# Pooled attention and a d_ff block on one core: the first two batches transposed on TensorE, first loads in another order, the first output phase in four banks

## The chip, the cores and the metric

The kernel runs on one NeuronCore of a Trainium2 chip. The metric is the device time of one execution in microseconds, the median of three runs. Before the change it is 352.62 us (352.56 to 353.64).

The engines are TensorE (PE: matmuls; its weight loads are shown as PEld), VectorE (DVE), ScalarE (ACT), GpSimd (POOL) and SyncE (SP). Each works through its own instructions in program order. Here SP only issues DMAs, and POOL issues some of them beside its arithmetic.

## The reference

Eight batches, eight heads, 576 tokens, head dimension 64; d_model 512 and d_ff 2048. Inputs and output are float32.

```python
k_p = k.reshape(B, H, 72, 8, D).mean(axis=3)      # pooled by 8 along the tokens
v_p = v.reshape(B, H, 72, 8, D).mean(axis=3)
scores = q @ k_p.T / sqrt(D)                      # 576 x 72 per batch and head
attn = softmax(scores)
x = (attn @ v_p), as 4608 x 512 (token, head*64+d)
h = x @ w_in                                      # 4608 x 2048
out = (h - tanh(h)) @ w_out                       # 4608 x 512
```

## The kernel before, in words

**Attention of one batch.** `load_kv` and `load_q` bring float32 rows into SBUF. `pool_kv` adds the eight token rows of a pool in three halvings; k's last step writes `kd`, a bf16 tile that holds every pooled row twice side by side, and v's last step multiplies with a block mask into `VB`. `q_prep` casts q to bf16 (L102 the 512 main tokens, L105 the last 64) and turns it with five DMA transposes (L109) into `qT`, where the head dimension lies on the partitions. `k_transpose` turns `kd` by matmuls with an identity operand into PSUM and copies it into `KB` (L167), a block layout with heads of even index on partitions 0 to 63 (copied by DVE) and of odd index on 64 to 127 (copied by ACT). `scores` multiplies `KB` with `qT` in two halves of 288 tokens and takes the exponential on ACT (L191). `av` multiplies a block of 128 tokens of it with `VB` (L208), whose last column per head gives the denominator; DVE takes its reciprocal (L217) and scales (L218) into `x_sb`; a DMA transpose (L226) writes that into `xT`, the input of the second part, with d_model on the partitions.

**The d_ff part** goes over nine groups of 512 tokens. Phase one, `mlp_h`, has sixteen steps, one per 128 columns of d_ff: four matmuls with 512 columns into an `hT_ps` bank (L256), tanh on ACT (L264), and the subtraction on DVE into a bf16 tile `gT` (L266). Phase two, `mlp_o`, has four blocks of 128 tokens (`tb`), each with four quarters (`qd`) of four matmuls (L276) that add into one `o_ps` bank; at the end of a block ACT copies it out (L285), and SP stores it. A batch has 576 tokens, a group 512, so group g needs the tokens of batches up to g alone.

**Order.** The schedule is manual: every engine runs its instructions in the order in which the program lists them. Ahead of the groups stand the loads of batch 0 on SP, identity, mask and memsets, `pool_kv(0)` with k on DVE and v on POOL, the cast loads of both weight matrices from POOL's queue (four pieces of `w1`, L322, then four of `w2`, L326), `q_prep(0)`, the loads of batch 1 on SP, and scores and `av` of batch 0. Inside group g the attention of batch g+1 is spread: its pooling on POOL at step 1, `q_prep` and the loads of batch g+2 at step 3, `k_transpose` at step 13, the five `scores` in the first five quarters of phase two, and the five `av` behind quarters 6, 7, 9, 10 and 12. SP's queue therefore holds, in order: loads of batch 0, q transposes of batch 0, loads of batch 1, x transposes of batch 0, and so on.

**PSUM** has eight banks: three for `hT_ps`, two for `o_ps`, and three (`ps_a`) that k transposes, scores and `av` share.

Of the kernel before, what the change touches and what calls it, by code (L numbers as in the profile page):

```python
# [33 lines left out]
def kernel(  # L34
# [64 lines left out]
    def q_prep(b):  # L99
        t = q_raws.pop(b)  # L100
        q_bf = work.tile([128, R + 1, H, D], BF16, name="q_bf", tag="q_bf")
        nc.vector.tensor_copy(  # L102
            out=q_bf[:, 0:R, :, :].rearrange("p j h d -> p h j d"), in_=t[:, :, 0:R, :]
        )
        nc.vector.tensor_copy(out=q_bf[:QT, R, :, :], in_=t[:QT, :, R, :])  # L105
# [9 lines left out]
    def pool_kv(b, ke, ve):  # L115
        kr = k_raw[b % 2].rearrange("p t (j d) -> p t j d", d=D)
        vr = v_raw[b % 2].rearrange("p t (j d) -> p t j d", d=D)
        kd = work.tile([128, NT, 2, D], BF16, name="kd", tag="kd")
        for eng, r in ((ke, kr), (ve, vr)):
            eng.tensor_tensor(  # L120
                out=r[:, :, 0:4, :], in0=r[:, :, 0:4, :], in1=r[:, :, 4:8, :], op=ALU.add
            )
            eng.tensor_tensor(  # L123
                out=r[:, :, 0:2, :], in0=r[:, :, 0:2, :], in1=r[:, :, 2:4, :], op=ALU.add
            )
            if r is kr:
                eng.tensor_tensor(  # L127
                    out=kd[:, :, :, :],
                    in0=r[:, :, 0:1, :].to_broadcast([128, NT, 2, D]),
                    in1=r[:, :, 1:2, :].to_broadcast([128, NT, 2, D]),  # L130
                    op=ALU.add,
                )
            else:
                eng.tensor_tensor(
                    out=r[:, :, 0, :], in0=r[:, :, 0, :], in1=r[:, :, 1, :], op=ALU.add
                )
                eng.tensor_tensor(  # L137
                    out=VB[b % 2][:, :, :, 0:D],
                    in0=r[:, :, 0:1, :].to_broadcast([128, NT, 3, D]),
                    in1=mask[:, :, :, :].to_broadcast([128, NT, 3, D]),  # L140
                    op=ALU.mult,
                )
        kdups[b] = kd

    def k_transpose(b):
        kd = kdups.pop(b)
        kb = KB[b % 2]
        for half in range(2):
            ps = ps_a.tile([128, 4, G], FP32, name="kT_ps", tag="ps_a")
            flat = ps.rearrange("p h g -> p (h g)")  # L150
            c = half * 4 * G
            while c < (half + 1) * 4 * G:
                t = c // 128
                n = min((t + 1) * 128, (half + 1) * 4 * G) - c
                nc.tensor.matmul(  # L155
                    flat[:, c - half * 4 * G : c - half * 4 * G + n],
                    lhsT=kd[:, t, :, :].rearrange("p a d -> p (a d)"),
                    rhs=ident[:, c - t * 128 : c - t * 128 + n],
                    start=True,
                    stop=True,  # L160
                )
                c += n
            for par, eng in ((0, nc.vector.tensor_copy), (1, nc.scalar.copy)):
                for i in range(2):
                    hp = half * 2 + i
                    hh = 2 * hp + par
                    eng(  # L167
                        out=kb[par * D : (par + 1) * D, hp, hh * G : (hh + 1) * G],
                        in_=ps[par * D : (par + 1) * D, 2 * i + par, :],
                    )  # L170
# [4 lines left out]
    def scores(b, t):  # L175
# [24 lines left out]
    def av(b, blk):  # L200
# [3 lines left out]
        x_sb = work.tile([128, 2, 4, D], BF16, name="x_sb", tag="x_sb", bufs=3)  # L204
        for half in range(2):
            ps = ps_a.tile([128, 4, D1], FP32, name="x_ps", tag="ps_a")
# [9 lines left out]
            rden = work.tile([128, 4, 1], FP32, name="rden", tag="rden", bufs=3)  # L216
# [71 lines left out]


    load_kv(0)  # L290
    load_q(0)
    make_identity(nc, ident)
    nc.gpsimd.memset(mask[:, :, :, :], 1.0)
# [7 lines left out]
        pattern=[[2 * G - 2 * G - 16 + 0, NT], [-G, 3]],  # L301
# [7 lines left out]
        base=G - 1 - G,  # L309
# [3 lines left out]
    for i in range(2):  # L313
        nc.vector.memset(k_raw[i][64:128, 4, :], 0.0)
        nc.vector.memset(v_raw[i][64:128, 4, :], 0.0)
        nc.vector.memset(KB[i][:, :, :], 0.0)
        nc.gpsimd.tensor_scalar_mul(VB[i][:, :, :, D:D1], mask[:, :, :, :], float(POOL))


    pool_kv(0, nc.vector, nc.gpsimd)  # L320
    for c in range(4):
        nc.gpsimd.dma_start(  # L322
            out=w1b[:, :, c * 512 : (c + 1) * 512], in_=w1_src[:, :, c * 512 : (c + 1) * 512]
        )
# [4 lines left out]
    q_prep(0)  # L329
    load_kv(1)  # L330
    load_q(1)
    k_transpose(0)
    for t in range(NT):
        scores(0, t)
    for blk in range(5):
        av(0, blk)


    for g in range(NG):
        nb = g + 1 if g + 1 < B else None  # L340
        gts = []
        for i in range(NHID):
            mlp_h(g, i, gts)
            if nb is not None:
                if i == 1:
                    pool_kv(nb, nc.gpsimd, nc.gpsimd)
                if i == 3:
                    q_prep(nb)
                    if nb + 1 < B:
                        load_kv(nb + 1)  # L350
                        load_q(nb + 1)
                if i == 13:
                    k_transpose(nb)
        for tb in range(4):
            for qd in range(4):
                mlp_o(g, tb, qd * 4, qd * 4 + 4, gts)
                u = tb * 4 + qd
                if nb is not None:
                    if u < NT:
                        scores(nb, u)  # L360
                    if u in (6, 7, 9, 10, 12):
                        av(nb, (6, 7, 9, 10, 12).index(u))
# [30 lines left out]
```

## Time and profile before

| | |
|---|---|
| median of 3 runs | 352.62 us (352.56 to 353.64) |
| the profiled execution's own time | 351.93 us |
| its span, first to last instruction | 350.2 us |
| PE busy | 287.7 us, 82% of the span |
| DVE, ACT, POOL busy | 166.7, 139.9, 106.9 us |
| first `hT` matmul of group 0 | 58.98 us |
| first `hT` matmul of group 1 | 94.44 us |
| mean granted TensorE clock | 0.961 |
| loads of one batch, page's issue part | k, v, q: 1152 KB each |
| weights | 4 pieces of 512 KB each in bf16 (twice that read as float32) |
| moved by DMA | 51.68 MB, of it 36.70 read from HBM |

All rows come from one profiled execution; times in them are microseconds from the start of the span. An arrow in a row's last part names what ended the idle time in front of that instruction. A matmul's end is modelled, so a busy PE is not PE at its peak; the distance between starts is the safer figure. The chain of waits is followed back from the last instruction: at each step to what released it.

### The profile page before, as it was taken

To read this page: it belongs to the slowest core of one execution; us is meant where nothing else is said; L and a number is where in the kernel's file an instruction comes from. 1 tells how busy PE (TensorE), PEld (TensorE's weight loads), DVE (VectorE), ACT (ScalarE), POOL (GpSimd) and SP (SyncE) were. 2 spreads that over 40 slices of the span, in tenths; PEclk is the share of its full clock that TensorE was granted. 3 is DMA by queue.
4 is the path that set the end of the run, shared out by engine and by line. 5 is a ranking of instruction groups with operands and counts; after the bars stand their busy time and mean duration, and the time that the engine had idled before them with its cause. 6 is when DMAs were issued, how large, how long until landed. Compare 5 with 4: busy or idle time off the path is not lost.

```text
span 350.2 us, 4472 instructions
## 1 busy us (share of the span) xinstructions
PE 287.7 (82%) x1538; PEld 143.3 (41%) x1568; DVE 166.7 (48%) x361; ACT 139.9 (40%) x293; POOL 106.9 (31%) x72
## 2 busy tenths in 40 slices
PE   0007002899989998999999899989998999999994
PEld 0004001345535543554455345535544554444442
DVE  6603002672485448355725772485458265703800
ACT  0023000464266246615551664266246615514611
POOL 2790940006800940193049007700940000000000
PEclk9999655899999999999999999999999999999999
DMA  6689995069827953892497469627952032012023
GB/s 240 179 139 282 265 219 98 16 121 329 171 73 212 286 119 69 259 254 83 104 321 169 95 176 311 146 48 232 281 104 67 22 89 79 2 60 61 2 51 69
DMA packets 71446, 51.68 MB, mean 148 GB/s; under 512 B 45312, under 2 KB 57600, under 8 KB 71424
## 3 DMA queue, kind: packets, MB, share of 16 engines
q1 hardware_dynamic: 67200, 47.20, 50.2%
q0 software_dynamic: 4224, 4.19, 7.4%
q8 instruction: 12, 0.20, 0.2%
q14 instruction: 10, 0.08, 0.1%
HBM read 36.70 MB, written 9.44 MB: 132 GB/s over the span
## 4 chain that ended last, share of the span: by engine, by line
PE 75%; DMA 9%; SPq 7%; DVE 5%; issue 2%; ACT 1%; ACTq 0%; DVEq 0%
PE o_ps L276 35%; PE hT_ps L256 31%; DMA xT<-x_sb 6%; PE s_ps L184 4%; PE x_ps L208 4%; SPq L91 3%; DMA q_raw<-in_q_dram 3%; DVE q_bf L102 3%; SPq L109 2%; DVE gT L266 2%; ACT t_sb L264 1%; SPq L79 1%; SPq L83 1%; DVE q_bf L105 1%; PE kT_ps L155 1%
## 5 line engine op out<-in xcount | busy, mean ns | idle before, releaser
L256 PE MATMUL hT_ps<-xT,w1b 128*128 128x512 bf16 x563 | 129.8, 384 | 9.5 <-DVE gT L266 6.2
L276 PE MATMUL o_ps<-w2b,gT 128*128 128x512 bf16 x559 | 134.6, 379 | 0.9
L266 DVE TENSOR_TENSOR gT<-hT_ps,t_sb 128x512 bf16<-128x512 f32 x144 | 97.5, 688 | 67.2 <-ACT t_sb L264 67.2
L264 ACT ACTIVATE t_sb<-hT_ps 128x512 f32<-128x512 f32 x144 | 85.2, 597 | 72.1 <-PE hT_ps L256 71.9
L256 PEld LDWEIGHTS <-w1b 128*128 128x128 bf16 x576 | 56.3, 99 | 78.2 <-issue 14.4
L276 PEld LDWEIGHTS <-gT 128*128 128x128 bf16 x576 | 53.9, 98 | 53.2
L120 POOL TENSOR_TENSOR k_raw<-k_raw 128x1280 f32<-128x1280 f32 x7 | 20.2, 2888 | 138.9 <-DMA k_raw<-in_k_dram 138.9
L285 ACT COPY o_sb<-o_ps 128x512 f32<-128x512 f32 x36 | 21.1, 586 | 92.7 <-PE o_ps L276 80.9
L217 DVE RECIPROCAL rden<-x_ps 128x4 f32<-128x4 f32 x80 | 14.2, 177 | 67.8 <-PE x_ps L208 67.3
L218 DVE TENSOR_TENSOR x_sb<-x_ps,rden 128x256 bf16<-128x256 f32 x80 | 34.0, 425 | 25.4 <-DMA xT<-x_sb 22.9
L208 PE MATMUL x_ps<-VB,E 128*128 128x130 bf16 (+2 forms) x240 | 22.2, 228 | 21.0 <-DVE x_sb L218 20.7
L184 PE MATMUL s_ps<-qT,KB 128*128 128x288 bf16 x128 | 23.6, 305 | 16.4 <-DMA qT<-q_bf 16.4
L191 ACT ACTIVATE E<-s_ps 128x288 bf16<-128x288 f32 x80 | 28.9, 412 | 17.0 <-PE s_ps L184 16.6
L208 PEld LDWEIGHTS <-E 128*128 128x128 bf16 x240 | 17.5, 101 | 31.2 <-DVE x_sb L218 22.4
L120 POOL TENSOR_TENSOR v_raw<-v_raw 128x1280 f32<-128x1280 f32 x8 | 23.1, 2886 | 8.4 <-DMA v_raw<-in_v_dram 8.3
L184 PEld LDWEIGHTS <-KB 128*128 128x128 bf16 x128 | 13.2, 103 | 27.3 <-issue 8.7
L137 POOL TENSOR_TENSOR VB<-v_raw,mask 128x960 bf16<-128x960 f32 x8 | 14.4, 1794 | 0.6
L123 POOL TENSOR_TENSOR v_raw<-v_raw 128x640 f32<-128x640 f32 x8 | 13.1, 1642 | 0.6
L155 PE MATMUL kT_ps<-ident,kd 128*128 128x128 bf16 (+3 forms) x48 | 3.7, 213 | 10.3 <-DVE kd L127 10.3
L102 DVE CAST q_bf<-q_raw 128x2048 bf16<-128x2048 f32 x8 | 10.2, 1271 | 3.2 <-DMA q_raw<-in_q_dram 3.2
L123 POOL TENSOR_TENSOR k_raw<-k_raw 128x640 f32<-128x640 f32 x7 | 10.8, 1536 | 0.6
L127 POOL TENSOR_TENSOR kd<-k_raw 128x640 bf16<-128x640 f32 x7 | 10.8, 1536 | 0.5
(24 smaller groups left out, 41.4 us busy)
## 6 DMA issues: line engine op xcount, KB each, us to landing
k_raw<-in_k_dram SPq DMA_DIRECT2D x8, 1024.0 KB, 6.1
v_raw<-in_v_dram SPq DMA_DIRECT2D x8, 1024.0 KB, 8.5
q_raw<-in_q_dram SPq DMA_DIRECT2D x8, 1024.0 KB, 10.9
out_dram<-o_sb SPq DMA_DIRECT2D x40, 128.0 KB, 2.4
out_dram<-o_sb SPq DMA_DIRECT2D x16, 256.0 KB, 2.6
w1b<-in_moe_w_in_dram POOLq DMA_DIRECT2D x4, 512.0 KB, 11.6
w2b<-in_moe_w_out_dram POOLq DMA_DIRECT2D x4, 512.0 KB, 26.9
k_raw<-in_k_dram SPq DMA_DIRECT2D x8, 128.0 KB, 6.1
```

The costliest lines, as they stand in the source:

```text
L102: nc.vector.tensor_copy(out=q_bf[:, 0:R, :, :].rearrange("p j h d -> p h j d"), in_=t[:, :, 0:R, :])
L120: eng.tensor_tensor(out=r[:, :, 0:4, :], in0=r[:, :, 0:4, :], in1=r[:, :, 4:8, :], op=ALU.add)
L123: eng.tensor_tensor(out=r[:, :, 0:2, :], in0=r[:, :, 0:2, :], in1=r[:, :, 2:4, :], op=ALU.add)
L184: nc.tensor.matmul(ps[:, :], lhsT=KB[b % 2][:, hp, t * 128 : (t + 1) * 128], rhs=qT[:, hp, half * hs : (half + 1) * hs], start=(n == 0), s ...
L191: nc.scalar.activation(out=E[:, t, half * hs : (half + 1) * hs], in_=ps[:, :], func=ACT.Exp, scale=SCALE)
L208: nc.tensor.matmul(ps[:, h0 : h0 + s1 - s0, :].rearrange("p h d -> p (h d)"), lhsT=E[:, t, c0 : c0 + 128], rhs=vb[:, t, s0:s1, :].rearrang ...
L218: nc.vector.tensor_tensor(out=x_sb[:, half, :, :], in0=ps[:, :, 0:D], in1=rden[:, :, :].to_broadcast([128, 4, D]), op=ALU.mult,)
L256: nc.tensor.matmul(h_ps[:, :], lhsT=w1b[:, fb, i * 128 : (i + 1) * 128], rhs=xT[:, fb, tok0 : tok0 + TG], start=(fb == 0), stop=(fb == NFB ...
L264: nc.scalar.activation(out=t_sb[:, :], in_=h_ps[:, :], func=ACT.Tanh)
L266: nc.vector.tensor_sub(out=gT[:, :], in0=h_ps[:, :], in1=t_sb[:, :])
L276: nc.tensor.matmul(o_ps[:, :], lhsT=gts[i][:, tb * 128 : (tb + 1) * 128], rhs=w2b[:, i, :], start=(i == 0), stop=(i == NHID - 1),)
L285: nc.scalar.copy(out=o_sb[:, :], in_=o_ps[:, :])
```

## The change

It has five parts.

1. **Loads of batch 0.** k in three pieces (two tiles, two tiles, the half tile), then q in two halves of four heads and its tail, then v in three pieces. Pooling follows the pieces: k on DVE in two parts (tiles 0 and 1; 2 to 4), v on DVE in two parts (0 to 2; 3 and 4). A one-element exponential stands at ACT's start. Some memsets go from DVE to POOL; `KB` has a padded, flat layout, which lets `k_transpose` copy two heads with one instruction (two copies per half instead of four).
2. **Batches 0 and 1 transposed by matmuls.** `q_pe_transpose` and `q_pe_tail` turn q with the identity as moving operand (4 matmuls of 128 columns per pair of heads, one 128x512 copy out of PSUM, in turn on DVE and ACT); `x_pe_transpose` does so for `x_sb` (4 matmuls, one copy on ACT). For these batches the scores are 512 tokens wide with a common tail of 64 (`scores_wide`, `scores_tail`). Batches 2 to 7 keep the DMA transposes, which then wait for nothing new. Before group 0, PSUM tiles come from all eight banks in turn (`ps_any`).
3. **Gate.** The two k loads of batch 1 wait for the third piece of `w1`. On SP the loads of q and v of batch 1 stand behind them, and behind those the loads of batch 2 (k, v, q), which stood at step 3 of group 0 before.
4. **Group 0.** Its sixteen `mlp_h` steps run with nothing between them. Then stand, in program order: pooling of k of batch 1 (POOL), the four `w2` loads (POOL), q cast and pooling of v of batch 1 (both DVE), k transposes and the first two q transposes of batch 1, and then phase two by quarters: the outer loop goes over quarters of d_ff, the inner over the four token blocks, in four banks (two `o_ps`, two `hT_ps`). Scores and `av` of batch 1 lie between.
5. **Groups 1 to 8.** Pooling at step 0 instead of 1, `k_transpose` behind the first quarter of phase two instead of step 13, `scores` behind quarters 1 to 5, `av` behind 7, 8, 9, 10 and 12. `q_bf` is one buffer instead of two, `x_sb` and `rden` have four instead of three.

The core of the diff:

```diff
+    KBW = NT * 128
+    KB = [const.tile([128, NHP * KBW + 2 * G + KBW], BF16, name=f"KB{i}") for i in range(2)]
+    q_bf = const.tile([128, R + 1, H, D], BF16, name="q_bf")
+    def ps_any(shape, dtype, name):
+        pool, tag = [(ps_a, "ps_a"), (ps_h, "hT_ps"), (ps_o, "o_ps")][
+            (0, 1, 2, 0, 1, 2, 0, 1)[rot[0] % 8]
+        ]
...
+    def evac(out, in_):
+        if evac_n[0] % 2:
+            nc.scalar.copy(out=out, in_=in_)
+        else:
+            nc.vector.tensor_copy(out=out, in_=in_)
+        evac_n[0] += 1
...
+    def q_pe_transpose(b, hps):
+        for hp in hps:
+            ps = ps_any([128, QA], FP32, "qT_ps")
+            for j in range(R):
+                nc.tensor.matmul(
+                    ps[:, j * 128 : (j + 1) * 128],
+                    lhsT=q_bf[:, j, 2 * hp : 2 * hp + 2, :].rearrange("p h d -> p (h d)"),
+                    rhs=ident[:, :], start=True, stop=True,
+                )
+            evac(qT[:, hp, 0:QA], ps[:, :])
...
+    def scores_wide(b, ts):
+        for t in ts:
+            ps = ps_any([128, QA], FP32, "s_ps")
+            score_mms(b, t, ps[:, :], 0, QA)
+            nc.scalar.activation(out=E[:, t, 0:QA], in_=ps[:, :], func=ACT.Exp, scale=SCALE)
...
+    def x_pe_transpose(b, blk, x_sb):
+        ps = ps_any([128, NFB, 128], FP32, "xT_ps")
+        for fb in range(NFB):
+            nc.tensor.matmul(
+                ps[:, fb, p0:128],
+                lhsT=xf[:, fb * 128 : (fb + 1) * 128],
+                rhs=ident[:, p0:128], start=True, stop=True,
+            )
+        nc.scalar.copy(out=xT[:, :, pos : pos + 128 - p0], in_=ps[:, :, p0:128])
...
-    load_kv(0)
-    load_q(0)
+    load_k(0, (0, 2, 4, 5))
+    load_q(0, 2)
+    load_v(0, (0, 2, 4, 5))
...
-    pool_kv(0, nc.vector, nc.gpsimd)
+    pool_k(0, nc.vector, 0, 2)
+    pool_k(0, nc.vector, 2, 5)
+    k_transpose(0, ps_any)
+    q_cast(0, 2, nc.gpsimd)
...
+    q_pe_transpose(0, (0, 1))
+    scores_wide(0, (0, 1))
+    q_pe_transpose(0, (2, 3))
+    q_pe_tail(0)
+    scores_wide(0, (2, 3, 4))
+    scores_tail(0)
+    pool_v(0, nc.vector, 0, 3)
+    pool_v(0, nc.vector, 3, 5)
+    for ld in load_k(1):
+        tc.add_manual_dep(
+            ld.ins,
+            w1_dmas[2].ins.name,
+            mybir.DependencyInfo(mybir.DependencyClass.Sync, mybir.DependencyReason.DATA),
+        )
+    load_q(1)
+    load_v(1)
+    pend = None
+    for blk in range(5):
+        x = av(0, blk, ps_any, False)
+        if pend is not None:
+            x_pe_transpose(0, *pend)
+        pend = (blk, x)
+    x_pe_transpose(0, *pend)
...
+    for i in range(NHID):
+        mlp_h(0, i, gts)
+    pool_k(1, nc.gpsimd)
     for c in range(4):
         nc.gpsimd.dma_start(
             out=w2b[:, c * 4 : (c + 1) * 4, :], in_=w2_src[:, c * 4 : (c + 1) * 4, :]
         )
...
+    q_cast(1)
+    pool_v(1, nc.vector)
+    load_k(2)
+    load_v(2)
+    load_q(2)
+    o_pools = [(ps_o, "o_ps"), (ps_o, "o_ps"), (ps_h, "hT_ps"), (ps_h, "hT_ps")]
...
+    k_transpose(1, ps_any)
+    q_pe_transpose(1, (0, 1))
+    for tb in range(4):
+        mlp_o(0, tb, 0, 4, gts, o_pools[tb])
+        if tb == 0:
+            scores_wide(1, (0,))
+            q_pe_transpose(1, (2,))
...
+    for qd in range(1, 4):
+        for tb in range(4):
+            mlp_o(0, tb, qd * 4, qd * 4 + 4, gts)
...
+            if qd >= 2 or tb >= 2:
+                if pend is not None:
+                    x_pe_transpose(1, *pend)
+                    pend = None
+                if blk < 5:
+                    pend = (blk, av(1, blk, ps_any, False))
+                    blk += 1
...
-                if i == 13:
-                    k_transpose(nb)
...
+                    if u == 0:
+                        k_transpose(nb, ps_b1)
+                    if 1 <= u <= NT:
+                        scores(nb, u - 1)
+                    if u in (7, 8, 9, 10, 12):
+                        av(nb, (7, 8, 9, 10, 12).index(u), ps_b1, True)
```

In group 0's phase two `ps_any` is bound to `ps_b1`, which takes tiles from `ps_a`'s three banks alone.

## Rows read from the trace of the kernel before

**Rows 1.** The page's slices (8.75 us each): busy tenths of PE.

```profile
PE   0007002899989998999999899989998999999994
```

**Rows 2.** Chain that ended last, from 25 to 95 us: start us, us, what.

```profile
25.59 10.63 SPq L91
...
36.31 19.11 DMA xT<-x_sb
...
58.98 0.58 PE hT_ps L256
...
76.88 0.86 PE o_ps L276 x4
...
86.11 0.35 PE x_ps L208 x6
...
94.44 3.47 PE hT_ps L256 x16
```

**Rows 3.** Timeline to 75 us: start, us, engine, line, instructions [idle before <-releaser].

```profile
6.98 1.49 DVE L120 TENSOR_TENSOR k_raw<-k_raw 128x1280 f32<-128x1280 f32 x1 [0.92 <-DMA k_raw<-in_k_dram]
8.51 0.82 DVE L123 TENSOR_TENSOR k_raw<-k_raw 128x640 f32<-128x640 f32 x1
...
10.25 0.66 PE L155 MATMUL kT_ps<-ident,kd 128*128 128x128 bf16 x6 [10.25 <-DVE kd L127]
11.12 2.88 POOL L120 TENSOR_TENSOR v_raw<-v_raw 128x1280 f32<-128x1280 f32 x1 [8.32 <-DMA v_raw<-in_v_dram]
13.43 1.64 DVE L102 CAST q_bf<-q_raw 128x2048 bf16<-128x2048 f32 x1 [3.24 <-DMA q_raw<-in_q_dram]
...
19.27 3.20 POOL L322 DMA_DIRECT2D w1b<-in_moe_w_in_dram  x4
...
21.66 0.89 SPq L79 DMA_DIRECT2D k_raw<-in_k_dram  x1
...
22.42 3.01 POOL L326 DMA_DIRECT2D w2b<-in_moe_w_out_dram  x4
...
32.07 0.18 DVE L217 RECIPROCAL rden<-x_ps 128x4 f32<-128x4 f32 x1 [14.77 <-PE x_ps L208]
...
32.63 0.17 DVE L217 RECIPROCAL rden<-x_ps 128x4 f32<-128x4 f32 x1
...
34.21 2.87 POOL L120 TENSOR_TENSOR k_raw<-k_raw 128x1280 f32<-128x1280 f32 x1 [8.78 <-DMA k_raw<-in_k_dram]
...
37.16 1.53 POOL L123 TENSOR_TENSOR k_raw<-k_raw 128x640 f32<-128x640 f32 x1
...
66.50 1.22 DVE L102 CAST q_bf<-q_raw 128x2048 bf16<-128x2048 f32 x1
...
67.63 0.41 DVE L105 CAST q_bf<-q_raw 64x512 bf16<-64x512 f32 x1
...
74.73 0.43 PE L155 MATMUL kT_ps<-ident,kd 128*128 128x128 bf16 x6
```

**Rows 4.** The page's groups by line: busy us, mean ns | idle before, releaser.

```profile
L256 PE MATMUL hT_ps<-xT,w1b 128*128 128x512 bf16 x563 | 129.8, 384 | 9.5 <-DVE gT L266 6.2
...
L266 DVE TENSOR_TENSOR gT<-hT_ps,t_sb 128x512 bf16<-128x512 f32 x144 | 97.5, 688 | 67.2 <-ACT t_sb L264 67.2
...
L285 ACT COPY o_sb<-o_ps 128x512 f32<-128x512 f32 x36 | 21.1, 586 | 92.7 <-PE o_ps L276 80.9
```

**Rows 5.** View by tile, the weights' DMAs: first w1b, then w2b.

```profile
DMA to landing us min/median/max: 6.2/11.6/18.7
...
DMA to landing us min/median/max: 22.1/26.9/31.2
```

**Rows 6.** Stretches: busy us of PE, PEld, DVE, ACT, POOL; clock; DMA share; GB/s.

```profile
37.00:38.00 1.00, 0.00 (x0) 0.00 (x0) 0.00 (x0) 0.00 (x0) 0.92 (x2) 0.51 1.12 290
...
92.60:125.30 32.70, 31.66 (x179) 16.12 (x181) 18.97 (x45) 15.76 (x34) 13.85 (x9) 1.00 0.64 177
```

**Rows 7.** Timeline of group 2 where its first phase turns into its second.

```profile
174.62 0.61 ACT L167 CAST KB<-kT_ps 64x72 bf16<-64x72 f32 x4 [1.08 <-DVE KB L167]
```

More of the change, by code (lines that the diff above doesn't have):

```diff
@@ L97, with q_cast, q_dma_transpose @@
     kdups = {}
-    def q_prep(b):
+    def q_cast(b, nh=1, tail=None):
         t = q_raws.pop(b)
[L101 to L105, printed above, removed]
+        n = H // nh
+        for i in range(nh):
+            nc.vector.tensor_copy(
+                out=q_bf[:, 0:R, i * n : (i + 1) * n, :].rearrange("p j h d -> p h j d"),
+                in_=t[:, i * n : (i + 1) * n, 0:R, :],
+            )
+        (tail or nc.vector).tensor_copy(out=q_bf[:QT, R, :, :], in_=t[:QT, :, R, :])
+    def q_dma_transpose(b):
         qT = work.tile([128, NHP, S], BF16, name="qT", tag="qT")
@@ L113, in q_prep @@
         qTs[b] = qT
[L115 to L121, printed above, removed]
-            )
[L123 to L143, printed above, removed]
@@ new lines, in q_pe_tail, with pool_k @@
+    def q_pe_tail(b):
+        ps = ps_any([128, NHP, QT], FP32, "qt_ps")
+        for hp in range(NHP):
+            nc.tensor.matmul(
+                ps[:, hp, :],
+                lhsT=q_bf[:, R, 2 * hp : 2 * hp + 2, :].rearrange("p h d -> p (h d)"),
+                rhs=ident[:, 0:QT],
+                start=True,
+                stop=True,
+            )
+        evac(qTs[b][:, :, QA:S], ps[:, :, :])
+    def pool_k(b, eng, t0=0, t1=NT):
+        r = k_raw[b % 2].rearrange("p t (j d) -> p t j d", d=D)[:, t0:t1, :, :]
+        if b not in kdups:
+            kdups[b] = work.tile([128, NT, 2, D], BF16, name="kd", tag="kd")
+        kd = kdups[b][:, t0:t1, :, :]
+        n = t1 - t0
+        eng.tensor_tensor(
+            out=r[:, :, 0:4, :], in0=r[:, :, 0:4, :], in1=r[:, :, 4:8, :], op=ALU.add
+        )
+        eng.tensor_tensor(
+            out=r[:, :, 0:2, :], in0=r[:, :, 0:2, :], in1=r[:, :, 2:4, :], op=ALU.add
+        )
+        eng.tensor_tensor(
+            out=kd,
+            in0=r[:, :, 0:1, :].to_broadcast([128, n, 2, D]),
+            in1=r[:, :, 1:2, :].to_broadcast([128, n, 2, D]),
+            op=ALU.add,
+        )
@@ L162, in k_transpose @@
                 c += n
+            step = KBW + 2 * G
             for par, eng in ((0, nc.vector.tensor_copy), (1, nc.scalar.copy)):
[L164 to L170, printed above, removed]
+                off = 2 * half * step + par * G
+                pr = slice(par * D, (par + 1) * D)
+                eng(
+                    out=kb[pr, off : off + 2 * step].rearrange("p (i x) -> p i x", x=step)[
+                        :, :, 0:G
+                    ],
+                    in_=ps[pr, :, par, :],
+                )
     E_tiles = {}
@@ L203, in av @@
         c0 = blk * 128 if blk < 4 else S - 128
[L204 removed]
+        x_sb = work.tile([128, 2, 4, D], BF16, name="x_sb", tag="x_sb", bufs=4)
         for half in range(2):
[L206 removed]
+            ps = alloc([128, 4, D1], FP32, "x_ps")
             for n, (t, s0, s1, h0) in enumerate(XM[half]):
```

180 lines of the change are left out of this document (132 added, 48 removed).

## The prediction

> **What bounds the kernel now.** I read the page's 40 slices first. PE shows 9 or 8 in nearly every slice from the seventh on, and almost nothing before it, so there are two regimes with different limits [rows 1]. The stretch of one middle group settles the second: PE is busy 31.66 of 32.70 us at a granted clock of 1.00, the upper of its two levels, 2.4 GHz [rows 6]. Inside it PE waits only for DVE: 6.2 us of idle over seven groups, 0.88 us each, behind the q cast [rows 4]. There PE is the bound, and only a change of PE's own work or of that wait matters.
>
> The chain of waits tells what the first regime is. The last steps before `hT` starts at 58.98 are no arithmetic: SP sits 10.63 us in one q-load issue (L91), and then a DMA transpose of `x_sb` takes 19.11 us to land [rows 2]. q had been there at 13.43 [rows 3]. So some 45 us go to queueing: batch 0's transposes share queue and engines with batch 1's loads and both weight matrices.
>
> **What the change removes there.** Batch 0 needs no DMA transpose any more, and the loads of batch 1 wait (on SP) for the third `w1` piece. I rebuild the start as a new chain.
>
> Loads: k, v and q, 3.5 MB, were in by 13.43 [rows 3]; k was in at 6.9, v at 11.1. Now k and q come first and v last, at about 13.5. The memsets (KB's is longer now) and the first exponential stand before that, where DVE still waited 0.92 us for k: nothing, or 1 us if the cover goes. DVE pools k in two parts. Its adds cost 1.49 us for 1280 and 0.82 for 640 elements [rows 3], so about 0.15 + 1.05 ns per element: the second part (three tiles: 768, 384, 384) takes 0.95 + 0.55 + 0.55 = 2.1 us from 6.95, to 9.0. PE's six k matmuls (0.66 us here, 0.43 for the same six at 74.73, [rows 3], so PE runs at its lower level this early) and the KB copies end at 10.3. The q casts in halves take to about 11.8 (1.64 us for the whole, [rows 3]). The q tail goes to POOL, 0.41 on DVE, 1.2 at POOL's rate (1.53 for 640 elements), and is wanted only at 15: nothing. Each of four transposed pieces is 4 matmuls and one 128x512 copy out of PSUM: 0.586 us on ACT by `o_sb`; on DVE 0.69, from `gT`'s row [rows 4]. ACT then has two such copies and five 512-wide exps, about 0.6 each, and a tail of 0.45. Interleaved as written, with 0.43 us for a 512-wide matmul (twice the 0.86 / 4 of [rows 2]), I get the last exp at 18.6. DVE pools v after its last copy, from 15.3: 2.6 + 1.95 = 4.55 us by the same slope, to 19.9. Ten half blocks of `x` at DVE's cadence, 32.63 − 32.07 = 0.56 us [rows 3], give 25.4. One transpose and the first `hT` matmul can start at 26.0, instead of 58.98.
>
> `w1`: POOL issued it at 19.27 before [rows 3]; now at about 12, after the q tail cast. Its first piece landed 6.2 us after its issue, so here near 18, well ahead of 26. Its last was issued 0.8 us before the end of that row, at 21.7, and landed by 21.7 + 18.7 = 40.4, the first at 25.5: five us apart [rows 5]. Without batch 1's loads beside it I take 3.8 (below), so the third lands near 26 and opens the gate.
>
> First phase of group 0: 76.88 − 58.98 = 17.9 us [rows 2], of which 0.88 was the wait for the cast and 0.43 k matmuls; 16 × 0.86 = 13.8 are the matmuls at the full clock (0.217 each from 3.47 / 16, [rows 2]). The rest, 2.8 us, is the low clock at the start. In the new chain PE is busy on and off from 11 to 26, so it may be up already; I charge half, 1.4. The phase ends at 26.0 + 13.8 + 1.4 = 41.2 (call it T).
>
> **What becomes late next.** Here the change puts work on a path. Behind the sixteen subtractions DVE has: the last of them (T + 1.4), batch 1's q cast 1.22 + 0.41, then the pooling of v, which moved from POOL to DVE (1.49 + 0.82 + 0.49 + 1.16 = 3.96), and only then the KB copies of batch 1, 0.3 on DVE and 0.3 on ACT. PE's second q transpose needs the PSUM buffer that these free, and all `o` matmuls stand behind it. So PE stands still until T + 7.6 = 48.8. The clock fell to its lower level, 1.2 GHz, by 37 to 38 [rows 6], when PE had been idle only since its last `x` matmuls, whose transpose was issued at 36.31 [rows 2]; so I charge a second slow start, 2.8.
>
> Then PE has 64 `o` matmuls (13.8), scores (eight 512 wide, 1.75, and the tail, 0.25), thirteen or so q transposes (0.75), five blocks of `x` at 0.35 (1.8, [rows 2]) and twenty x transposes (1.1): 19.4. The trace has no such transposes; 128 columns are 0.054 by the 512-wide rate, and 0.43 / 6 = 0.07 by the k matmuls, which would add 0.5. I take the first, since they stand among long matmuls. Each x transpose waits for DVE: two halves (1.1 us) plus the hand-over against the 0.86 us of one `o` quarter before it, some 0.4, five times: 2.0. Sum 7.6 + 2.8 + 19.4 + 2.0 = 31.8; `hT` of group 1 starts at 73.0 instead of 94.44 [rows 2]. Gain 21.4 us.
>
> Is the data there? Gate 26, k of batch 1 about 33 (with the rest of `w1` beside it), POOL's pooling 2.87 + 1.53 + 1.53 [rows 3] to 39, and behind it `w2`'s issue. q and v of batch 1 follow at about 37 and 41, before DVE asks at 42.6 and 44.2. `w2` is needed in quarters at 48.8, about 57, 62 and 70, which is what the four banks do. Before, `w2`'s last piece was issued at 24.6 [rows 3] and landed 31.2 later, at 55.8, against 40.4 for `w1`'s last [rows 5]: 15.4 us for four, 3.8 each, beside loads and transposes. From 39 + 2 this gives 45 to 57: hidden, with 4 to 13 us of cover. On SP the gate also holds all of batch 1 and 2's loads; the first output goes out near 71, long after.
>
> The other end of that price is an even split of the start's rate: 3.5 MB by 13.43, the first issue at 0.8, is 280 GB/s; half of it for a piece that reads 1 MB is 7.5 us, and the last quarter would land near 71, one late. I keep 3.8, which had loads in the other queue too, and give the split a part in a rival. The Trainium skill (DMA: Bandwidth & Descriptors, Queues, rings and completion order) says that each DMA engine takes turns between queues, packet by packet, which speaks for the even split; by it alone the sum would be a microsecond higher.
>
> **The other groups.** The k transposes go from the thirteenth `hT` step to the first `o` quarter. PE then needs KB 0.86 us after them. DVE is free at 1.5 us into the phase, and ACT's copies wait for DVE's [rows 7]; with two copies per half instead of four I get KB's first half 2.1 us in, against PE's need at 2.0: a stall of 0.15, seven times, +1.0 (ends: 0, and +3.2 if a score waits for both halves). The q cast at step 3, the DMA transposes and the 0.88 stay. Group 1's first `hT` steps need two banks that the `o` blocks held, and ACT frees one per 0.59 us [rows 4], faster than PE's 0.86: nothing. `av` one quarter later, and four buffers instead of three, lie beside 0.86 us quarters: nothing. Pooling one step earlier is POOL's alone: nothing.
>
> **Sum.** 351.93 (the profiled execution: span 350.2 and 1.7 around it) − 21.4 + 1.0 = 331.5. The median, 352.62, lies 0.7 above the profiled one, so I say 332.
>
> **Rivals.**
> *Late transfers* (0.18): batch 1's k took 34.21 − 21.66 = 12.5 us in the crowd. If it does after the gate, `w2` is issued near 45, v lands near 47, KB is 4 us later, and at the even split `w2`'s last quarter comes about 45 + 2 + 30 = 77, seven us late: 336 to 342. For it: 7 MB queued at once behind the gate. Against: no DMA transposes, and `w1` nearly done.
> *Quicker* (0.20): the clock is up at both starts (−1.4, −2.8), x transposes wait less (−2), the first chain is 1.5 us shorter: 323 to 327. Against: 7 us of PE standing still.
> *Not early at all* (0.03): the start stays bound by transfers, `hT` begins no earlier than 45: about 345 to 352. Against: `w1` first piece, 6.2 us after issue.
> *Slower* (0.04): the software queue that carries `w2` gets its turn only when batch 1 and 2's loads are through and is slowed by each later issue; as every `o` bank needs every quarter, PE then stands in the first output phase. It decides from where `w2`'s last quarter lands after 91 (group 1 would start after 94.44): 50 us after issue, against the longest of 31.2 [rows 5]. At 55 us it would cost 5: 357.
> *Forecast* (0.55): 327 to 336, centre 332.
>
> **Numbers.** The forecast's range joined with quicker and most of late transfers: 323 to 341. A difference under 0.3% can't be told from none. Faster 0.95, same 0.01, slower 0.04.
>
> **What would show it.** Right: first `hT` near 26; the third `w1` piece and then k's issue near 26; PE idle some 6 us after the first phase, released through KB's copies and DVE's pooling of v; group 1's `hT` near 73; 32.7 to 33.1 us per group after. Wrong: PE's idle there ended by `w2`'s DMA (late transfers); a granted clock of 1.0 through 40 to 50 (quicker); a KB wait of over 0.5 us per group.

## The result, and the profile after

The changed kernel takes 333.5 us (median of 4 runs, 332.39 to 333.65) against 352.59 us (4 runs, 352.36 to 353.64): a ratio of 0.9446, 95% interval 0.9419 to 0.9474. The prediction said 332, with a range of 323 to 341. The profiled execution took 333.65 us with a span of 331.9. An execution over 1.5% above the fastest of its kernel is left out of the times and ratios (there is one, of `e3_no_gate`, with 340.18 us).

The page's slices of the changed kernel, busy tenths of PE in 8.3 us each, answer to [rows 1]:

```profile
PE   0769707998999899989998999899989999999994
```

Two empty slices are left where there were five: the first, and the sixth, 41.5 to 49.8 us. The chain of waits (start us, us, what) shows what lies in the sixth; it answers to [rows 2]:

```profile
25.25 13.83 PE hT_ps L370 x64
...
40.34 1.22 DVE q_bf L131
41.55 0.33 DVE q_bf L135
41.88 1.41 DVE v_raw L197
43.31 3.40 DVE v_raw L200
46.73 1.72 DVE v_raw L203
48.47 2.37 DVE VB L206
...
51.15 0.28 ACT KB L235
51.47 0.59 PE qT_ps L154 x4
52.06 1.71 PE o_ps L391 x4
...
57.54 0.86 PE o_ps L391 x4
...
75.31 3.57 PE hT_ps L370 x16
...
108.19 3.47 PE hT_ps L370 x16
...
140.97 3.47 PE hT_ps L370 x16
```

From the first `hT` matmul to the end no DMA stands in the chain. The first phase runs from 25.25 without a gap. Then DVE's four v steps take 8.9 us (41.88 to 50.8), KB's copies follow, and only they let PE go on at 51.47. The first `o` quarters take 1.71 us instead of 0.86. Group 1 starts at 75.31, and the groups follow at 32.8 us each (140.97 − 108.19 = 32.78; 32.88 for the first).

The timeline of the changed kernel shows POOL beside DVE in that stretch, and the issue on SP that the gate held (start, us, engine, line, instructions, idle before); it answers to [rows 3] and [rows 7]:

```profile
22.06 0.37 SPq L99 DMA_DIRECT2D k_raw<-in_k_dram  x1
...
29.20 2.91 POOL L181 TENSOR_TENSOR k_raw<-k_raw 128x1280 f32<-128x1280 f32 x1 [14.52 <-DVE gT L380]
...
30.23 0.69 DVE L380 TENSOR_TENSOR gT<-hT_ps,t_sb 128x512 bf16<-128x512 f32 x1 [0.17 <-ACT t_sb L378]
...
42.37 3.65 POOL L181 TENSOR_TENSOR k_raw<-k_raw 128x1280 f32<-128x1280 f32 x1 [4.06 <-DMA k_raw<-in_k_dram]
43.31 3.39 DVE L200 TENSOR_TENSOR v_raw<-v_raw 128x640 f32<-128x640 f32 x1
46.10 1.99 POOL L184 TENSOR_TENSOR k_raw<-k_raw 128x640 f32<-128x640 f32 x1
...
124.64 0.49 ACT L235 CAST KB<-kT_ps 64x144 bf16<-64x144 f32 x2 [0.96 <-DVE KB L235]
...
124.97 0.17 PEld L254 LDWEIGHTS <-KB 128*128 128x128 bf16 x2 [0.43 <-ACT KB L235]
```

POOL's wait for batch 2's k ended at 42.37, and it began to add it while DVE added batch 1's v. A 640-element add took DVE 3.39 us; it was 0.82 in [rows 3]. It ended at 46.70, 0.7 us behind the end of POOL's first add at 46.02: most of its time passed beside that one instruction. Not everything on DVE is held so: the subtractions, which read one operand from PSUM, kept 0.69 us beside POOL's adds of batch 1's k (29.20 to 35.3).

Landing times of `w1` and then `w2` in the changed kernel (issue to landing, us), against [rows 5]:

```profile
DMA to landing us min/median/max: 5.5/8.0/10.7
...
DMA to landing us min/median/max: 11.1/16.4/21.2
```

`w2`, issued from 35.3, landed between 46.4 and 58.7, before PE asked for it. Single microseconds of the changed kernel, against [rows 6]; the granted clock is the third figure from the right:

```profile
22.00:23.00 1.00, 1.00 (x13) 0.87 (x11) 0.93 (x5) 0.59 (x1) 0.00 (x0) 0.52 1.25 209
23.00:24.00 1.00, 0.74 (x12) 0.53 (x10) 0.93 (x5) 0.58 (x1) 0.00 (x0) 1.00 1.23 207
...
43.00:44.00 1.00, 0.00 (x0) 0.00 (x0) 0.97 (x2) 0.00 (x0) 1.00 (x1) 0.72 1.13 282
...
57.00:58.00 1.00, 1.00 (x12) 0.67 (x11) 0.54 (x1) 0.79 (x2) 1.00 (x1) 0.95 0.37 58
```

The clock was up before the first phase, fell in the stand behind it, and came back at 57: for 5.6 us from 51.5 on PE worked at half its pace.

### The profile page after: what moved, and what is told of

The parts are those of the page before. It is cut to its first block, busy times and chain, and to the rows that moved or that the text cites. A ratio compares the mean times of both kernels' runs of the same rounds, so it can differ in the third digit from the quotient of the medians.

```text
span 331.9 us, 4575 instructions
## 1 busy us (share of the span) xinstructions
PE 296.3 (89%) x1648; PEld 147.9 (45%) x1648; DVE 179.6 (54%) x363; ACT 147.7 (44%) x285; POOL 99.7 (30%) x69
## 4 chain that ended last, share of the span: by engine, by line
PE 80%; DVE 13%; issue 2%; ACT 2%; DMA 1%; SPq 0%; DVEq 0%; ACTq 0%
PE o_ps L391 37%; PE hT_ps L370 33%; PE s_ps L254 4%; PE x_ps L305 4%; DVE q_bf L131 3%; DVE x_sb L315 3%; DMA k_raw<-in_k_dram 1%; DVE gT L380 1%; DVE v_raw L200 1%; ACT t_sb L378 1%; PE s_ps L289 1%; DVE v_raw L197 1%; DVE VB L206 1%; DVE rden L314 1%; DVE v_raw L203 1%
## 5 line engine op out<-in xcount | busy, mean ns | idle before, releaser
L391 PE MATMUL o_ps<-w2b,gT 128*128 128x512 bf16 x576 | 140.2, 382 | 0.0
L370 PE MATMUL hT_ps<-xT,w1b 128*128 128x512 bf16 x576 | 126.9, 379 | 5.3 <-DVE gT L380 5.3
L181 POOL TENSOR_TENSOR k_raw<-k_raw 128x1280 f32<-128x1280 f32 x7 | 21.0, 2999 | 133.0 <-DMA k_raw<-in_k_dram 118.5
L261 ACT ACTIVATE E<-s_ps 128x288 bf16<-128x288 f32 x60 | 21.4, 410 | 9.7 <-PE s_ps L254 9.7
L197 POOL TENSOR_TENSOR v_raw<-v_raw 128x1280 f32<-128x1280 f32 x6 | 18.2, 3040 | 0.0
L254 PE MATMUL s_ps<-qT,KB 128*128 128x288 bf16 x96 | 16.7, 287 | 0.0
L154 PE MATMUL qT_ps<-ident,q_bf 128*128 128x128 bf16 x32 | 4.2, 291 | 12.7 <-ACT KB L235 9.5
L235 ACT CAST KB<-kT_ps 64x144 bf16<-64x144 f32 x16 | 3.9, 273 | 24.5 <-DVE KB L235 24.5
L254 PEld LDWEIGHTS <-KB 128*128 128x128 bf16 x96 | 9.2, 98 | 9.1 <-ACT KB L235 2.6
L184 POOL TENSOR_TENSOR k_raw<-k_raw 128x640 f32<-128x640 f32 x7 | 11.2, 1601 | 0.5
L206 POOL TENSOR_TENSOR VB<-v_raw,mask 128x960 bf16<-128x960 f32 x6 | 10.8, 1794 | 0.5
## 6 DMA issues: line engine op xcount, KB each, us to landing
q_raw<-in_q_dram SPq DMA_DIRECT2D x7, 1024.0 KB, 11.5
out_dram<-o_sb SPq DMA_DIRECT2D x16, 256.0 KB, 2.5
```

Of the source, the lines that this page charges most:

```text
L181: eng.tensor_tensor(out=r[:, :, 0:4, :], in0=r[:, :, 0:4, :], in1=r[:, :, 4:8, :], op=ALU.add)
L197: eng.tensor_tensor(out=r[:, :, 0:4, :], in0=r[:, :, 0:4, :], in1=r[:, :, 4:8, :], op=ALU.add)
L254: nc.tensor.matmul(ps[:, :], lhsT=KB[b % 2][:, hp * KBW + t * 128 : hp * KBW + (t + 1) * 128], rhs=qT[:, hp, half * hs : (half + 1) * hs], ...
L261: nc.scalar.activation(out=E[:, t, half * hs : (half + 1) * hs], in_=ps[:, :], func=ACT.Exp, scale=SCALE)
L370: nc.tensor.matmul(h_ps[:, :], lhsT=w1b[:, fb, i * 128 : (i + 1) * 128], rhs=xT[:, fb, tok0 : tok0 + TG], start=(fb == 0), stop=(fb == NFB ...
L391: nc.tensor.matmul(o_ps[:, :], lhsT=gts[i][:, tb * 128 : (tb + 1) * 128], rhs=w2b[:, i, :], start=(i == 0), stop=(i == NHID - 1),)
```

## The experiments

All have the changed kernel as their base and are timed against the kernel before on the same chip; the ratio is given with its 95% interval. Medians of the kernel before lie between 351.8 and 352.6 us, so two kernels timed on different chips are compared by their ratios (0.01 is 3.5 us). Line numbers in their rows are those of the changed kernel as far as the edits don't shift them.

**Where the start's gain comes from: order, or matmuls in place of DMA transposes?** `e4_dma_turned_b0`:

```diff
-    q_pe_transpose(0, (0, 1))
-    scores_wide(0, (0, 1))
-    q_pe_transpose(0, (2, 3))
-    q_pe_tail(0)
-    scores_wide(0, (2, 3, 4))
+    q_dma_transpose(0)
+    scores_wide(0, (0, 1, 2, 3, 4))
...
+    for blk in range(5):
+        av(0, blk, ps_any, True)
     (gated load_k(1), load_q(1), load_v(1) behind them; no x_pe_transpose)
```

> Batch 0's q and x go by DMA transposes again, but SP holds the loads of batch 1 behind them (with the gate as it is), so no load stands ahead of a transpose. It tells order apart from the matmul transposes. If the queue's order was all that cost 33 us at the start: the five q transposes cost some 4 us more than matmuls, the x transposes some 2.5, first hT at 30 to 33, and the time rises by 3 to 7 us over the changed kernel, to 337 to 341. Rival (the w1 load that runs at that time slows the transposes as the crowd did before, 19 us): first hT at 38 or later, time over 345.

348.29 us, ratio 0.9900 (0.9866 to 0.9934). The rival holds. Its timeline:

```profile
11.21 7.28 SPq L141 DMA_TRANSPOSE qT<-q_bf  x5
...
26.94 3.60 PE L289 MATMUL s_ps<-qT,KB 128*128 128x512 bf16 x16 [17.30 <-DMA qT<-q_bf]
...
39.14 16.18 PE L370 MATMUL hT_ps<-xT,w1b 128*128 128x512 bf16 x64 [6.25 <-DMA xT<-x_sb]
```

The q transposes were issued from 11.2 and the first score had its operand at 26.9, with no batch load ahead of them; the only other traffic then was the rest of v and `w1`. Most of the transposes in this trace land 2.4 us after their issue; one of these took 11.5. That the traffic beside them is the reason isn't shown by itself. So a right order on SP alone starts `hT` at 39.1, 20 us before the kernel before and 14 us after the changed one. Most of that 20 us does not show in the time: the gated loads now start at 38.7, `o` starts at 68.1 (76.88 before) and group 1 at 90.2 (94.44 before). (Batch 1's q pieces swap their copying engine here, since the turn of DVE and ACT begins anew; that moves no wait above.)

**Does the gate do anything?** `e3_no_gate`:

```diff
-    for ld in load_k(1):
-        tc.add_manual_dep(ld.ins, w1_dmas[2].ins.name, ...)
+    load_k(1)
```

> Batch 1's k loads don't wait for w1's third piece. If the gate is what keeps the weights in time: w1 lands five us a piece as before, the first phase waits for it, w2 comes later, and the time rises by 2 to 6 us. Rival (the gate is idle, since the first phase needs w1 only from 25 us on, at 3.5 us a piece): first hT still at 25.1, PE held as before by DVE's v pooling; and as batch 2's k then lands before DVE starts on v of batch 1, POOL's pooling overlaps less with it and the time falls by 1 to 5 us.

338.6 us (three runs, 334.42 to 339.2), ratio 0.9585 (0.9516 to 0.9655): about 5 us slower than with the gate. The profiled execution was the quickest, less than 1 us above the changed kernel, and shows `w1` at its edge:

```profile
36.40 3.63 PE L370 MATMUL hT_ps<-xT,w1b 128*128 128x512 bf16 x16 [0.34 <-DMA w1b<-in_moe_w_in_dram]
```

The last piece landed 21.9 us after its issue, at 36.36, just as step 12 asked; with the gate the longest was 10.7. The other two took 4 to 5 us longer, and no trace shows what held them; a `w1` still later would, and that is not shown. The gate is worth its place all the same, and in this trace its effect is to keep `w1` in front.

**Why did DVE take 8.9 us for what was put at 4.0?** `e2_k2_last`:

```diff
-    load_k(2)
     load_v(2)
     load_q(2)
+    load_k(2)
```

> Only the order of batch 2's loads changes: v, q, k instead of k, v, q, so that POOL's pooling of batch 2's k can't start until k has landed last, some 8 us later, and DVE pools batch 1's v alone. If DVE's v pooling took 9.0 us instead of the predicted 4.0 because POOL pooled k of batch 2 at the same time (42.4 to 49.8), it takes 4.0 here, KB's copies come at 45.9, o starts near 46.6, and the time falls by 4.5 to 5.5 us, to 328 to 329. Rival (these DVE instructions are that slow after the DMAs or at this place for another reason): DVE's pooling still takes 8 to 9 us and the time stays within 1 us of 333.5.

328.19 us, ratio 0.9321 (0.9298 to 0.9345). Its chain:

```profile
41.91 1.41 DVE v_raw L197
43.34 0.84 DVE v_raw L200
44.20 0.50 DVE v_raw L203
44.73 1.16 DVE VB L206
46.19 0.28 ACT KB L235
46.51 0.58 PE qT_ps L154 x4
```

The same four instructions take 3.9 us once POOL's k adds come later (its next one starts at 58.76), and PE goes on at 46.51 instead of 51.47. The 5 us reach the end: 5.3 by the medians, 4.4 by the ratios. The DMA engines were as busy as before in that stretch (1.17 from 43 to 44, against 1.13), so their traffic isn't the reason: it was POOL at the same time, not DVE's work.

**Take v's pooling off DVE.** `e1_v1_on_pool`:

```diff
-    pool_v(1, nc.vector)
+    pool_v(1, nc.gpsimd)
```

> Batch 1's v is pooled on POOL, behind the issue of w2, instead of on DVE; nothing else changes. My theory: PE's stand from 42.0 to 51.5 us is DVE's v pooling (9.0 us), so KB's copies then come right after the q cast (41.9), o starts near 42.8, hT of group 1 at 65 to 67 instead of 75.1, and the time falls by 8 to 10 us, to 324 to 326. Rival (w2's transfer would have held PE in any case): w2's first piece lands at 46.4 and its last at 58.7, so o starts near 46.5 and the gain is 4 to 6 us. Second rival (the v pooling on POOL, beside nothing on DVE, is late for batch 1's av): the wait moves to av near 52, gain under 5 us.

327.06 us, ratio 0.9291 (0.9267 to 0.9314): 5.5 us less than the changed kernel by the ratios (6.4 by the medians), and `o` starts with `w2`'s first piece, at 46.07, so the first rival is right. Chain, then timeline:

```profile
35.12 10.91 DMA w2b<-in_moe_w_out_dram
46.07 1.86 PE o_ps L391 x4
```

```profile
40.32 1.83 DVE L131 CAST q_bf<-q_raw 128x2048 bf16<-128x2048 f32 x1
...
42.08 1.75 DVE L135 CAST q_bf<-q_raw 64x512 bf16<-64x512 f32 x1
```

With DVE's pooling gone the next wait is `w2`, 1.6 us behind KB's copies. And the q tail's cast took 1.75 us instead of 0.41, beside POOL's adds: DVE is held by POOL again, now with POOL on v and DVE on its casts.

**Give `w2` the DMA engines to itself.** `e5_second_gate` is `e1_v1_on_pool` and

```diff
+    w2_dmas = []
...
+    for ld in load_k(2):
+        tc.add_manual_dep(ld.ins, w2_dmas[2].ins.name, ...)
-    load_k(2)
```

> As e1_v1_on_pool, and batch 2's k loads wait for w2's third piece, so that batch 2's q and v stand behind them too. In e1_v1_on_pool the first o matmul waited for w2's first piece, which landed 10.9 us after its issue at 35.1. If that was because batch 2's loads had been queued since 29 us, the first piece lands 5 to 7 us after its issue, near 41, and then KB's copies (about 42.5) release PE: o starts near 43, hT of group 1 near 65.5 instead of 68.7, the time falls 3 us below e1_v1_on_pool, to 324. Rival (w2 is slow beside batch 1's q and v, or by itself): it lands near 45 to 46 again and the time stays within 1 us of 327. A risk for both: batch 2's loads, out from about 47, have to be in by 69 for the q cast of group 1.

326.35 us, ratio 0.9288 (0.9261 to 0.9314), no more than `e1_v1_on_pool`. The first piece did land 6.3 us after its issue, at 41.8, as the theory had it. But the end does not see it:

```profile
38.47 2.93 POOL L197 TENSOR_TENSOR v_raw<-v_raw 128x1280 f32<-128x1280 f32 x1
...
40.31 2.19 DVE L131 CAST q_bf<-q_raw 128x2048 bf16<-128x2048 f32 x1
41.48 2.41 POOL L200 TENSOR_TENSOR v_raw<-v_raw 128x640 f32<-128x640 f32 x1
42.42 1.75 DVE L135 CAST q_bf<-q_raw 64x512 bf16<-64x512 f32 x1
...
45.18 1.91 PE L391 MATMUL o_ps<-w2b,gT 128*128 128x512 bf16 x4
```

The casts took 3.9 us beside POOL, and the clock had gone down at 43. The expected 3 us had turned into a wait for DVE, which I had left out of the sum.

**Are the four banks needed?** `e7_blocks_in_order` is `e1_v1_on_pool` and

```diff
-        mlp_o(0, tb, 0, 4, gts, o_pools[tb])
+        mlp_o(0, 0, tb * 4, tb * 4 + 4, gts)
...
-            mlp_o(0, tb, qd * 4, qd * 4 + 4, gts)
+            mlp_o(0, qd, tb * 4, tb * 4 + 4, gts)
```

> As e1_v1_on_pool, but group 0's second phase goes block by block through all of d_ff in the two o banks, as before the change, with the attention steps of batch 1 at the same places. PE then needs w2's last piece in the fourth step instead of the thirteenth. If the quarters in four banks are what hides w2 (pieces land at about 46, 50, 54, 57 to 59 here): o starts at 46.1, stands for w2's later pieces until about 57 to 59, and the time rises by 4 to 7 us over e1_v1_on_pool, to 331 to 334. Rival (the attention steps between the quarters give w2 enough time): within 1 us of 327.

335.09 us, ratio 0.9534 (0.9515 to 0.9553): 8 us over `e1_v1_on_pool`, more than the 4 to 7 expected. PE waits for each of `w2`'s pieces, 5.9 us in four waits (1.0 us in one wait in `e1_v1_on_pool`). A further part is the clock, which stayed down to about 54 instead of 50. The last wait:

```profile
59.16 1.02 PE L391 MATMUL o_ps<-w2b,gT 128*128 128x512 bf16 x4 [2.24 <-DMA w2b<-in_moe_w_out_dram]
```

**The later groups.** `e6_old_places` puts `k_transpose` back to step 13, `scores` to the quarters 0 to 4 and `av` to 6, 7, 9, 10, 12:

```diff
+                if i == 13:
+                    k_transpose(nb, ps_b1)
...
-                    if u == 0:
-                        k_transpose(nb, ps_b1)
-                    if 1 <= u <= NT:
-                        scores(nb, u - 1)
-                    if u in (7, 8, 9, 10, 12):
+                    if u < NT:
+                        scores(nb, u)
+                    if u in (6, 7, 9, 10, 12):
```

> In groups 1 to 8 the k transposes go back to step 13, the scores to the first five quarters and av to quarters 6, 7, 9, 10, 12, as before the change; the start is the changed kernel's. If the new places cost PE 0.10 us per group (KB late for the first score, as the trace of the changed kernel shows at 124.97), the span from group 1's first hT to the end falls from 256.6 to about 255.9 and the time by 0.7 us. Rival (the new places pay, because the old ones put KB's copies between tanh and subtraction): it rises by 0.5 to 1.5 us.

331.83 us (330.76 to 333.49), ratio 0.9436 (0.9413 to 0.9460), which the times can't tell from the changed kernel's. Its trace has 256.0 us from group 1's first `hT` (73.06) to the end, against 331.9 − 75.31 = 256.6: 0.5 us, near the 0.7 expected.

`e8_cast_in_pieces` cuts the cast of batches 2 to 7:

```diff
-                if i == 3:
-                    q_cast(nb)
-                    q_dma_transpose(nb)
+                if i in (1, 3, 5, 7, 9):
+                    q_piece(nb, (i - 1) // 2)      # one j: cast, then its DMA transpose
+                if i == 9:
                     if nb + 1 < B:
                         load_k(nb + 1)
```

> The changed kernel with the q cast of batches 2 to 7 cut into five pieces (four of 512 elements and the tail) at steps 1, 3, 5, 7 and 9, each with its DMA transpose right behind, and the loads of the next batch at step 9. It tests the reading that PE's 0.88 us of idle per group are DVE's backlog from 1.6 us of cast at one place: each piece (about 0.37) is worked off in two steps of 0.17 us slack, so the idle goes and the time falls by 5 us (6 x 0.88), to 328 to 329. Rival (the backlog is there in any case, or the later loads and transposes hold the first scores): less than 2 us, or slower.

326.85 us, ratio 0.9287 (0.9265 to 0.9309). Chain:

```profile
139.00 8.20 PE hT_ps L383 x38
...
202.48 8.20 PE hT_ps L383 x38
```

Two groups in 202.48 − 139.00 = 63.48 us, 31.74 each instead of 32.78: the 0.88 us are gone, and 0.16 more, which no row explains.

**The q cast of batch 1 ahead of the turn.** `e9_cast_early` is `e5_second_gate` with

```diff
         mlp_h(0, i, gts)
+        if 10 <= i <= 14:
+            (cast j = i - 10 of batch 1's q, on DVE)
...
-    q_cast(1)
```

> As e5_second_gate, with batch 1's q cast taken out of the turn between the phases: five pieces behind steps 10 to 14 of group 0's first phase. In e5_second_gate w2's first piece was there at 41.8, but DVE's q cast took 3.9 us beside POOL's v pooling instead of 1.6, so that o started at 45.2 with the clock down since 43. If that cast is now the limit: KB's copies come at about 41, o starts near 42 when w2 lands, the clock stays up (PE idle under 3 us), hT of group 1 comes near 63 instead of 68.3, and the time falls by 4.5 to 5.5 us below e5_second_gate, to 321. Rival (the clock falls all the same, or q of batch 1 lands after 35 and the pieces hold the subtractions): 1 to 2.5 us.

328.42 us, ratio 0.9333 (0.9300 to 0.9366): no faster than `e5_second_gate`, and by the ratios 1.6 us slower, though the intervals just overlap. Both theories missed. The timeline:

```profile
37.10 3.06 POOL L489 DMA_DIRECT2D w2b<-in_moe_w_out_dram  x4
37.96 0.41 DVE L483 CAST q_bf<-q_raw 128x512 bf16<-128x512 f32 x1
...
38.90 4.46 DVE L483 CAST q_bf<-q_raw 128x512 bf16<-128x512 f32 x1
...
40.15 2.91 POOL L197 TENSOR_TENSOR v_raw<-v_raw 128x1280 f32<-128x1280 f32 x1
```

A cast that takes 0.41 us elsewhere in this trace began while POOL issued `w2` and ended at 43.36, 0.3 us after POOL's add: it waited out that add. The issue alone is no sufficient reason, since the cast at 37.96 ran beside it in 0.41 us; what held the later one from 38.90 to the start of the add at 40.15 stays open. One thing came as the rival had it: an earlier piece took 1.32 us beside POOL's adds, a subtraction came late, and PE stood 0.66 us in the first phase. The Trainium skill (SBUF — State Buffer, Who interferes with whom) says that DVE and GpSimd share a pair of SBUF ports, that whichever comes first holds it for the whole instruction, that two-port casts ask for it, and that a DVE add with both inputs in SBUF contends with a GpSimd instruction that reads SBUF. The rows here and in `e2_k2_last` agree in that DVE is held while POOL adds: 0.41 against 4.46 us, 3.9 against 8.9.

**No POOL work beside DVE at the turn.** `e11_v1_later` is the changed kernel with the second gate and

```diff
     q_cast(1)
-    pool_v(1, nc.vector)
...
             scores_wide(1, (tb,))
+    pool_v(1, nc.vector)      # behind the first four o quarters
```

> The changed kernel with two edits: batch 2's k loads wait for w2's third piece (as in e5_second_gate), and DVE pools v of batch 1 only after the first four o quarters of group 0, while POOL stands idle (batch 2's k isn't there before 55). In e9_cast_early a DVE cast of 0.4 us took 4.5 us while POOL first issued w2 and then pooled v; so the point is to have no POOL work beside DVE at the turn. If that is right: q cast 1.6 us from 40.3, KB's copies at 42.4, o from about 43, clock still up, v's pooling 4.0 us from about 47.5, hidden behind o quarters, hT of group 1 near 64, time 322 to 323. Rival (the clock has fallen by 43 as in e5_second_gate): 325. Rival (av waits for v's pooling on DVE): 326.

324.37 us, ratio 0.9223 (0.9198 to 0.9248), 8 us below the changed kernel by the ratios. Timeline:

```profile
42.30 1.22 DVE L131 CAST q_bf<-q_raw 128x2048 bf16<-128x2048 f32 x1
43.43 0.41 DVE L135 CAST q_bf<-q_raw 64x512 bf16<-64x512 f32 x1
...
44.69 1.03 PE L391 MATMUL o_ps<-w2b,gT 128*128 128x512 bf16 x4
```

Casts and copies take their own time, and the `o` quarters run at full speed from the start (1.03 us with the modelled end, 1.91 in `e5_second_gate`). `o` starts 1.7 us later than expected, and this execution's clock came up only at 28 (below), which cost its first phase 1.5 us.

**All together.** `e10_all` adds the edits of `e8_cast_in_pieces` and `e6_old_places` to `e9_cast_early`, `e12_all` adds them to `e11_v1_later`.

> e9_cast_early together with the q cast of batches 2 to 7 in pieces (e8_cast_in_pieces, 6.2 us of span) and the old places of k transposes, scores and av (e6_old_places, 0.7 us). If these lie in separate stretches, they add: 321 - 6.2 - 0.7 = 314. Rival (the k transposes at step 13 meet DVE's backlog from the pieces at steps 7 and 9, or the later loads of the next batch come late): 316 to 318.

> e11_v1_later with the q cast of batches 2 to 7 in pieces (6.2 us) and the old places of k transposes, scores and av (0.7 us): 322.5 - 6.9 = 315.5, or 318 with either rival of e11_v1_later.

320.61 us, ratio 0.9113 (0.9082 to 0.9143), and 316.21 us (316.10 to 317.13), ratio 0.8995 (0.8976 to 0.9014). Both add up from their parts (328.4 − 6.9 = 321.5; 324.4 − 6.9 = 317.5). `e12_all` is the fastest of all, 16 us below the changed kernel by the ratios. Its slices:

```profile
PE   0659969989999999999999999999999999999994
```

## Why the prediction was right

The point that mattered was right: the first regime is bound by queueing and not by arithmetic, and without it a chain of DVE, PE and ACT work sets the start. `e4_dma_turned_b0` narrows it: of the 34 us by which `hT` starts earlier, the order of the loads gives 20, and 14 need batch 0's transposes off the DMA queues. Step by step:

| step | predicted | measured |
|---|---|---|
| first `hT` of group 0 | 26.0 | 25.1 |
| gate opens | 26 | 22.1 |
| low clock in the first phase | 1.4 | 0 |
| end of the first phase, T | 41.2 | 38.9 |
| DVE's pooling of batch 1's v | 3.96 | 8.9 |
| PE goes on | 48.8 | 51.5 |
| from there to group 1's `hT` (slow start, work, waits) | 24.2 | 23.8 |
| group 1's first `hT` | 73.0 | 75.3 |
| from group 1's `hT` to the end, more than before | +1.0 | +0.8 |
| profiled execution | 331.5 | 333.65 |

(The next to last: 331.9 − 75.31 = 256.6 against 350.2 − 94.44 = 255.8.)

One term was mis-sized: "the pooling of v, which moved from POOL to DVE (1.49 + 0.82 + 0.49 + 1.16 = 3.96)". `e2_k2_last` measures it: 3.9 alone, 8.9 beside POOL. I had taken each instruction's price from a stretch in which POOL was idle, and the prediction never asks when batch 2's k lands and what POOL does once `w2` is issued. The prediction had a row of its own that warned: the q cast took 1.64 us beside POOL's add of v and 1.22 later [rows 3]. I used both numbers and didn't ask why they differ. The 5 us were offset by 2.3 that the start and the first phase gained (0.9 and 1.4) and by 0.6 in the last steps, so the sum came out 2 us low. That it came so near is in part luck: the errors happened to point in opposite ways.

The charge for a second slow start, 2.8, was right in place and size. PE stood from 39.3, with four transposes at 41.6, the clock fell in the 43 to 44 stretch, and 5.6 us at half the pace are 2.8 us lost. The first charge, 1.4, was not: of the twelve profiled executions whose start PE works through alike (all but `e4_dma_turned_b0`), ten had the clock up by 24.2, before the first `hT`, and paid nothing. In `e10_all` it came up at about 25.7, and only `e11_v1_later` paid as much as charged: its clock stood at 0.50 until 28 and its first phase took 15.3 us instead of 13.8. What decides it, no run shows.

The prediction says that PE "runs at its lower level this early", from 0.66 against 0.43 us for the same six matmuls. The granted clock in that stretch (10 to 11 us, kernel before) reads 1.00. In the changed kernel it reads 1.00 too from 12 to 13, where three 512-wide matmuls in a row take 1.44 us, about twice what they take later (0.65). So there the pace speaks for the lower level and the granted figure doesn't show it.

Of the rivals, *late transfers* did not come: `w2` landed at 46.4 to 58.7 (predicted 45 to 57), ahead of the moved need. That agreement is luck: its issue began at 35.3 instead of 39, and its last piece landed 23.4 us after that instead of 18, so a piece cost more than the 3.8 us that I kept and less than the 7.5 of an even split. `e1_v1_on_pool` and `e7_blocks_in_order` show how close it was: let `o` become ready 5.4 us earlier and `w2` is the bound; take the four banks away and it costs 8 us. *Quicker* was right in one of its terms, the clock of the first phase, and in part in another (the first chain was 0.9 us shorter, not 1.5). *Not early at all* has its answer in `e4_dma_turned_b0`: with DMA transposes kept for batch 0, and the gated loads behind them, the time is 348. The KB wait in the later groups was sized right (PE's weights waited until 124.97, some 0.1 us; 0.15 predicted).

That the q cast costs PE 0.88 us in every group was read from the rows and left as it is by the change; `e8_cast_in_pieces` shows that 6 us were to be had there, the most that any edit of the later groups won here.

## What to carry to other kernels

Price an instruction from a stretch in which the other engines do what they will do at its new place: DVE adds and casts that read SBUF took up to eleven times their own time beside POOL's adds here, while subtractions with one operand in PSUM took no longer. Moving work from DVE to POOL (`e1_v1_on_pool`) did not end that: the casts that stayed on DVE were then the ones held. Having the two work at different times did (`e2_k2_last`, `e11_v1_later`). When a wait is taken away, list what ends next and by how much; here KB, `w2` and the casts stood within 5 us of each other, and each single edit won only the distance to the next. A burst of 1.6 us on an engine with 20% slack (DVE's 0.69 of every 0.86 us in the first phase) was better cut in pieces.

## What the runs showed of the hardware that I had not expected

- A DVE cast of 128x512 (0.41 us) that started beside POOL's DMA issue lasted 4.46 us, to just behind the following POOL add, though one that ran wholly beside the issue took 0.41 (`e9_cast_early`); plain adds of 640 elements went from 0.82 to 3.39 us, while POOL's own 1280-element add only went from 2.9 to 3.65 (changed kernel). Subtractions on DVE with an operand in PSUM kept 0.69 us beside POOL's adds.
- DMA transposes with no batch load ahead of them, beside the rest of v and a cast-load of weights, were still slow: five of them, issued from 11.2, had their first reader wait until 26.9, and one took 11.5 us to land, against 2.4 us for most in that trace (`e4_dma_turned_b0`).
- The same start had its clock up at 23 in one execution and at 28 in another (22 to 23 at 0.52 and then 1.00 in the changed kernel; 0.50 through 27 to 28 in `e11_v1_later`), worth 1.5 us.
